# Moving the transpose of the softmax sums by one step in an attention and MLP kernel

## The chip, the cores and the metric

The kernel runs on one core of a Trainium2 chip. The metric is device time in microseconds (us) of one execution. Engines are named as in the profile: PE (TensorE matmul), PEld (TensorE weight load), DVE (VectorE), ACT (ScalarE), POOL (GpSimd), SP (SyncE, whose queue issues nearly all DMAs here).

## The reference, cut to what matters

Attention over 4 batches, 8 heads, 576 positions and head size 64, with a bias that a small network computes from the positions, and an MLP on the 2304 tokens:

```python
scores = q @ k.T / 8 + bias[head]              # 576 x 576 for each batch and head
attn = exp(scores - max(scores, axis=-1))
attn = attn / (attn.sum(axis=-1) + 1e-9)
x = concat_heads(attn @ v)                     # 2304 x 512
h = relu(x @ w_in)                             # w_in 512 x 2048
out = (s * h * h + b) @ w_out                  # w_out 2048 x 512
```

The division by the sums is what the change touches. The kernel multiplies the finished `attn @ v` by the reciprocals of the sums instead of dividing `attn`.

## The kernel before, in words

The work is written out in order by hand: every engine runs its instructions in the order of the program text, and so does SP's queue of DMAs. There are three stretches: the bias of all heads (up to about 60 us), attention (60 to 350 us), and the MLP.

**Pairs, units and steps.** Attention works on 16 pairs; a pair is one head of two batches. The query rows of a pair are five units: units 0 to 3 are 128 rows of both batches (x = 0, 1), unit 4 is the last 64 rows of both batches stacked to 128. One step per unit, `step(n)`, with n = 5p + u for pair p and unit u. A step does three things for three units. For unit n + 2: the scores (L228, PE into a PSUM tile for each x), `biased` (L242, DVE: subtract from the bias, and the row's minimum), and `expo` (L253, ACT: exp, which also adds up a column of the sums `su`). For unit n: `probs_t`, which transposes the exponentials on PE and copies them from PSUM. For pair p - 1: `av` (L333, L336), the product with v that accumulates in `xps`. The attended pair is therefore one pair behind the transposed one, and the scores are two units ahead of it. Because of this lead the scores that a step u = 3 computes are those of unit 0 of the next pair, and all nine columns of the sums of pair p are there by step u = 3.

**`probs_t` and its PSUM tiles.** Every call takes one of two buffers of `ps_t` (tile name `tps`, 128 x 512, one bank). A unit 0 to 3 has three calls: part 2 transposes a 128 x 128 block (L307, copied by ACT in L308), parts 0 and 1 transpose four blocks each (L298, copied by ACT in L303 and by DVE in L305). Unit 4 has two: part 1 transposes a block of 64 columns (L318, copied by two ACT instructions of L320), part 0 four blocks (L313, copied by DVE in L315).

**The sums.** In step u = 3 `norm` (L265, L266, DVE) adds 1e-9 and takes the reciprocal of the 128 x 9 sums, between the two `biased` of the step. `norm_t`, called at the end of part 2 of the same step, transposes the result on PE (L270) into the columns 128 to 255 of the tile whose columns 0 to 127 L308 has just been told to copy, and DVE copies it out (L272, tile `rt`). At the end of the step `norm_store` issues four small DMAs on SP (L278, L280) that write `rt` to device memory (`rs`), after the loads of the step (`load_be`, `load_q`, `load_k`). At the end of step u = 4 `norm_load` (L285) issues two DMAs that read each row back, repeated over 64 partitions (tile `rb`). `rb` is needed in step u = 4 of the next pair, where `av` of the previous pair ends: L341 (DVE) multiplies `xps` by `rb`, and L342 stores the result to `xt` in device memory.

**Filler.** After `av`, a step calls `fill` once (u odd) or twice (u even). Each call does one piece of decoding the MLP's weights: an ACT, a POOL or a DVE instruction (L373, L375, L377, L380, L383), at times a load of raw weights (L360) or a split (L392 to L395). In steps u = 0 and 1 POOL splits the next pair's q and k (L203, L204), which the scores of step u = 3 read.

**The end of attention.** Steps 78 and 79 (u = 3 and 4 of the last pair) and the steps 80 to 84, which only do `av` of the last pair, are mixed with the first work of the MLP: `att` is the next step, `xsp` a split of x (L419 ACT, L420 DVE), `h0` and `h1` the first two tiles of the MLP's first product (`expand`, L430 to L440):

```python
for work in (att, xsp, xsp, xsp, xsp, att, h0, att, h0, att,
             att, h1, wsp, wsp, att, h1, att, wsp, wsp):
    next(work)
pctx.close()
ps_ctx.close()
```

The PSUM tiles of the second product (`project`, L454) are allocated after that, in the room of `xps` and `tps`; so the first `project` comes after L341 of the last pair.

Of the kernel before, what the change touches and what calls it, by code (L numbers as in the profile page):

```python
# [26 lines left out]
def attention_moe(ctx, tc, q, k, v, w_in, w_out, dist, par, out):  # L27
# [14 lines left out]
    LAST = 5 * NP  # L42
# [144 lines left out]
    def load_q(p):  # L187
        if p < NP:
            h, b0 = pairs[p]
            qs[p] = io.tile([128, 640], F32, tag="qt", name="qt")  # L190
            nc.sync.dma_start(out=qs[p], in_=q[b0 // 2, h])

    def load_k(p):
        if p < NP:
            h, b0 = pairs[p]
            ks[p] = io.tile([128, S + 64], F32, tag="kt", name="kt")
            nc.sync.dma_start(out=ks[p], in_=k[b0 // 2, h])
# [16 lines left out]
    def scores(n):  # L214
        p, t = divmod(n, 5)
        qt, kt = qs[p], ks[p]
        c = slice(128 * t, 128 * t + 128)
        xs = range(width(n))
        ps = [ps_s.tile([128, 2, 512], F32, tag="s", name="sps") for _ in xs]
        mms = []  # L220
        for hf in range(2):
            for x in xs:
                d = slice(64 * x, 64 * x + 64) if t < 4 else slice(0, 128)
                o = hf * HALF + (64 if x == 0 else 0)
                for i, (a, b) in enumerate(((0, 0), (0, 1), (1, 0))):
                    mms.append((i, hf, x, ps[x][:, hf, 0:HALF], qt[d, a, c], kt[d, b, o:o + HALF]))
        for i, _, _, o, a, b in sorted(mms, key=lambda e: e[1::-1]):
            nc.tensor.matmul(o, a, b, start=(i == 0), stop=(i == 2))  # L228
        units[n] = (
            tp.tile([128, 2, S], F32, tag="pr", name="pr"),  # L230
            sm.tile([128, 2], F32, tag="mn", name="mn"),
            ps,
        )
        if t == 0:
            sums[p] = sm.tile([128, 9], F32, tag="su", name="su")

    def biased(n, x):
        p, t = divmod(n, 5)
        _, mn, ps = units[n]
        bias = bts[group[p]][:, t, 64 - 64 * x:64 - 64 * x + S] if t < 4 else bes[p]  # L240
        tt = tp.tile([128, S], F32, tag="tt", name="tt")
        nc.vector.tensor_tensor_reduce(  # L242
            tt.rearrange("p (a b) -> p a b", a=2), ps[x][:, :, 0:HALF],
            bias.rearrange("p (a b) -> p a b", a=2),
            -1.0 / ROOT, BIG, ALU.add, ALU.min, mn[:, x:x + 1],
        )
        tts[n, x] = tt

    def expo(n, x):
        p, t = divmod(n, 5)  # L250
        pr, mn, _ = units[n]
        col = 4 * x + t if t < 4 else 8
        nc.scalar.activation(  # L253
            pr[:, x], tts.pop((n, x)), AF.Exp, bias=mn[:, x:x + 1], scale=-1.0,
            accum_out=sums[p][:, col:col + 1])

    def width(n):
        return 2 if n % 5 < 4 else 1
# [4 lines left out]
    def norm(p):  # L263
        su = sums.pop(p)
        nc.vector.tensor_scalar(su, su, 1e-9, None, op0=ALU.add)  # L265
        nc.vector.reciprocal(su, su)  # L266
        rows[p] = su

    def norm_t(p, ps):
        nc.tensor.transpose(ps[0:9, 128:256], rows.pop(p), ident)  # L270
        rt = sm.tile([9, 128], F32, tag="rt", name="rt", bufs=2)
        nc.vector.tensor_copy(rt, ps[0:9, 128:256])  # L272
        rts[p] = rt

    def norm_store(p):
        rt = rts.pop(p)
        for x in range(2):
            nc.sync.dma_start(  # L278
                out=rs_d[p][x, 0:512].rearrange("(t j) -> t j", j=128), in_=rt[4 * x:4 * x + 4, :])
            nc.sync.dma_start(out=rs_d[p][x:x + 1, 512:S], in_=rt[8:9, 64 * x:64 * x + 64])  # L280

    def norm_load(p):
        rbs[p] = tp.tile([128, S], F32, tag="rb", name="rb", bufs=2)
        for x in range(2):
            nc.sync.dma_start(out=rbs[p][64 * x:64 * x + 64, :], in_=rs_d[p][x:x + 1, :].broadcast_to([D, S]))  # L285

    def probs_t(n, part):
        p, t = divmod(n, 5)
        pr = units[n][0]
        if p not in pts:  # L290
            pts[p] = (ptp.tile([128, 4, 2, S], F32, tag="pt", name="pt"),
                      ptp.tile([128, S], F32, tag="ptr", name="ptr"))
        pt, ptr = pts[p]
        ps = ps_t.tile([128, 512], F32, tag="t", name="tps")
        c = slice(128 * t, 128 * t + 128)
        if t < 4 and part < 2:
            for kb in range(4):
                nc.tensor.transpose(  # L298
                    ps[:, 128 * kb:128 * kb + 128],
                    pr[:, part, 64 * part + 128 * kb:64 * part + 128 * kb + 128], ident)  # L300
            o, i = pt[:, :, part, c], ps.rearrange("p (a b) -> p a b", a=4)
            if part == 0:
                nc.scalar.activation(o, i, AF.Copy)  # L303
            else:
                nc.vector.tensor_copy(o, i)  # L305
        elif t < 4:
            nc.tensor.transpose(ps[:, 0:128], pr.rearrange("p x j -> p (x j)")[:, 512:640], ident)  # L307
            nc.scalar.activation(ptr[:, c], ps[:, 0:128], AF.Copy)  # L308
            if t == 3:
                norm_t(p, ps)  # L310
        elif part == 0:
            for kb in range(4):
                nc.tensor.transpose(  # L313
                    ps[:, 128 * kb:128 * kb + 128], pr[:, 0, 128 * kb:128 * kb + 128], ident)
            nc.vector.tensor_copy(  # L315
                pt[:, :, :, 512:S], ps.rearrange("p (a x b) -> p a x b", a=4, x=2))
        else:
            nc.tensor.transpose(ps[0:64, 0:128], pr[:, 0, 512:S], ident)  # L318
            for x in range(2):
                nc.scalar.activation(  # L320
                    ptr[64 * x:64 * x + 64, 512:S], ps[0:64, 64 * x:64 * x + 64], AF.Copy)

    def av(p, kb, hf):
        h, b0 = pairs[p]
        pt, ptr = pts[p]
        vt = vals[p]
        if kb == 0 and hf == 0:
            accs[p] = ps_x.tile([128, 2, 512], F32, tag="x", name="xps")
        ps = accs[p]
        c = slice(hf * HALF, (hf + 1) * HALF)  # L330
        if kb < 4:
            for x in range(2):
                nc.tensor.matmul(ps[64 * x:64 * x + 64, hf, 0:HALF], vt[:, 4 * x + kb, :], pt[:, kb, x, c],  # L333
                                 start=(kb == 0), stop=False)
        else:
            nc.tensor.matmul(ps[:, hf, 0:HALF], vt[:, 8:10].rearrange("p i d -> p (i d)"), ptr[:, c],  # L336
                             start=False, stop=True)
        if kb == 4 and hf == 1:
            xs = rbs.pop(p)
            xv = xs.rearrange("p (a b) -> p a b", a=2)  # L340
            nc.vector.tensor_tensor(xv, ps[:, :, 0:HALF], xv, op=ALU.mult)  # L341
            nc.sync.dma_start(out=xt_d[b0 // 2][:, h * D:(h + 1) * D, :], in_=xs)  # L342
# [125 lines left out]
    def ok(n, x):  # L468
        return 0 <= n < LAST and x < width(n)
# [7 lines left out]
    def step(n):  # L477
        p, u = divmod(n, 5)
        m = n + 2
        cur = 0 <= n < LAST  # L480
        if ok(m, 0):
            scores(m)
            biased(m, 0)
        if cur and u == 3:
            norm(p)
        if ok(m, 1):
            biased(m, 1)
        if cur:
            for part in (2, 0, 1) if u < 4 else (1, 0):
                probs_t(n, part)  # L490
        if ok(m, 0):
            expo(m, 0)
        if ok(m, 1):
            expo(m, 1)
        if p >= 1:
            av(p - 1, u, 0)
            av(p - 1, u, 1)
            fill()
            if u % 2 == 0:
                fill()  # L500
        if 0 <= n < LAST:
            if u == 3:
                load_be(p + 1)
                load_q(p + 3)
                load_k(p + 3)
                norm_store(p)
            if u == 4:
                norm_load(p)
            if u < 2:
                split_qk(p + 1, u)  # L510
            if u == 4:
                load_v(p + 2)
            for e in loads_at.get((p, u), ()):
                load_bias(*e)
# [14 lines left out]
    def fill():  # L529
        next(filler, None)  # L530
# [77 lines left out]
    for e in late[0:4]:  # L608
        load_w(*e)
    att = map(step, range(LAST - 2, LAST + 5))  # L610
    xsp = map(lambda a: split_x(0, a), range(KB))
    wsp = map(lambda i: split_w(0, 1, i), range(4))
# [107 lines left out]
```

## Time and profile before

| | |
|---|---|
| median of 3 runs | 754.46 us (754.11 to 759.69) |
| profiled execution | 759.01 us, of which the core's span is 757.0 us |
| PE busy | 722.6 us, 95% of the span |
| DVE, ACT, POOL busy | 428.3, 362.5, 185.4 us |
| mean granted TensorE clock | 0.991 |
| chain that ended last | PE 81%, POOL 6%, DVE 5%, issue 4% |
| idle time of PE before L270 | 17.3 us in 16 instructions |

Starts are us from the span's start. A row of a timeline gives start, length, engine, line, operation, output<-input, how many instructions are merged, and in brackets the idle time of the engine before it and what ended it. The end of a matmul is modelled, and pipelined matmuls overlap in the rows; the distance between starts is the safer measure. A granted clock of 1.00 is 2.4 GHz, 0.5 is 1.2 GHz; a figure in between is a mixture of the two over the stretch.

### The profile page before, as it was taken

Reading aid. Unit: us, or ns where it says so; the run is one execution under the profiler, and the core shown is the slowest. Engines: PE = TensorE matmul, PEld = TensorE weight load, DVE = VectorE, ACT = ScalarE, POOL = GpSimd, SP = SyncE. Lnnn points to the kernel's source line nnn. Section 1 sums busy time; section 2 is a strip of 40 time slices with the busy share of each in tenths; the row PEclk is TensorE's granted clock in tenths of the full one; section 3 lists DMA queues with packets and bytes.
Section 4 is the critical chain, followed back from the end, with each engine's and each line's share of the span. In section 5 each row is a group of like instructions: output and inputs, shape, how many; then the busy total and the mean of one; then the engine's idle time right before and its main releaser. Section 6 shows DMA issues by size and latency. Waiting matters only on the chain.

```text
span 757.0 us, 12033 instructions
## 1 busy us (share of the span) xinstructions
PE 722.6 (95%) x4530; PEld 538.3 (71%) x4530; DVE 428.3 (57%) x794; ACT 362.5 (48%) x756; POOL 185.4 (24%) x194
## 2 busy tenths in 40 slices
PE   8978989898999999999999999999999999999998
PEld 5436666565666666666888888888888888888896
DVE  7966867687787877894369742233323333232332
ACT  7967656465666666664454432223222232222332
POOL 7990524344141252310755200000000000000000
PEclk9999999899999999999999999999999999999999
DMA  5878654545363664334012121000300002000100
GB/s 168 281 219 265 196 181 156 181 156 209 128 209 128 211 225 156 128 114 172 17 38 88 42 79 34 1 1 0 112 1 0 1 1 83 1 1 0 57 1 28
DMA packets 39817, 76.98 MB, mean 102 GB/s; under 512 B 9040, under 2 KB 12368, under 8 KB 39760
## 3 DMA queue, kind: packets, MB, share of 16 engines
q1 hardware_dynamic: 39616, 75.90, 30.7%
q8 instruction: 35, 0.57, 0.3%
q10 hardware_dynamic: 144, 0.33, 0.1%
q14 instruction: 22, 0.18, 0.1%
HBM read 55.45 MB, written 20.13 MB: 100 GB/s over the span
## 4 chain that ended last, share of the span: by engine, by line
PE 81%; POOL 6%; DVE 5%; issue 4%; DMA 2%; SPq 1%; ACT 1%; POOLq 0%; DVEq 0%
PE hps L430 26%; PE o L454 26%; PE sps L228 8%; PE xps L333 7%; PE tps L298 7%; POOL f L119 4%; DVE tt L242 3%; PE xps L336 2%; PE tps L307 1%; PE tps L313 1%; DMA raw<-in_moe_w_in_dram 1%; PE tps L318 0%; SPq L154 0%; DMA pt__110<-in_par_dram 0%; POOL kr L204 0%
## 5 line engine op out<-in xcount | busy, mean ns | idle before, releaser
L454 PE MATMUL o<-who,gt 128*128 128x512 f32 x576 | 192.4, 393 | 0.0
L430 PE MATMUL hps<-x,whi 128*128 128x512 f32 (+1 forms) x640 | 183.7, 371 | 0.0
L435 DVE SCALAR_TENSOR_TENSOR r<-r,sb 128x512 f32<-128x512 f32 (+1 forms) x80 | 56.7, 709 | 192.3 <-ACT r L434 192.3
L434 ACT ACTIVATE r<-hps 128x512 f32<-128x512 f32 (+1 forms) x80 | 44.5, 557 | 223.7 <-PE hps L430 223.7
L430 PEld LDWEIGHTS hps<-x,whi 128*128 128x128 f32 x640 | 116.9, 188 | 23.8 <-issue 0.4
L454 PEld LDWEIGHTS o<-who,gt 128*128 128x128 f32 x576 | 108.2, 188 | 24.2
L430 PE MATMUL hps<-x,wli 128*128 128x512 f32 (+1 forms) x320 | 118.7, 371 | 0.0
L253 ACT ACTIVATE pr<-tt,mn 128x576 f32<-128x576 f32 x144 | 110.2, 767 | 13.9 <-DVE mn L242 13.4
L242 DVE CUSTOM_DVE_ANT_0 tt<-sps,bt 128x576 f32<-128x576 f32 x128 | 92.3, 749 | 39.6 <-PE sps L228 34.8
L454 PE MATMUL o<-wlo,gt 128*128 128x512 f32 x288 | 113.2, 393 | 0.0
L228 PEld LDWEIGHTS sps<-kr,qr 64*128 64x128 f32 (+1 forms) x864 | 69.5, 187 | 42.1 <-DVE mn L242 16.9
L228 PE MATMUL sps<-kr,qr 64*128 64x288 f32 (+1 forms) x864 | 90.9, 313 | 6.5 <-POOL kr L204 2.9
L440 DVE SCALAR_TENSOR_TENSOR gt<-r,sb,gt 128x512 fp32r<-128x512 f32 (+1 forms) x80 | 56.3, 704 | 54.0 <-ACT gt L439 54.0
L298 PE MATMUL tps<-ident,pr 128*128 128x128 f32 x512 | 79.6, 285 | 0.9 <-ACT ptr L308 0.3
L439 ACT ACTIVATE gt<-r,sb 128x512 fp32r<-128x512 f32 (+1 forms) x80 | 54.4, 680 | 52.3 <-DVE r L435 52.3
L333 PE MATMUL xps<-pt,vt 128*64 128x288 f32 x512 | 78.4, 430 | 0.0
L298 PEld LDWEIGHTS tps<-ident,pr 128*128 128x128 f32 x512 | 58.5, 144 | 13.4 <-ACT ptr L308 9.0
L430 PEld LDWEIGHTS hps<-x,wli 128*128 128x128 f32 x320 | 60.1, 188 | 11.0
L454 PEld LDWEIGHTS o<-wlo,gt 128*128 128x128 f32 x288 | 54.1, 188 | 11.6
L305 DVE COPY pt<-tps 128x512 f32<-128x512 f32 x64 | 44.0, 688 | 17.4 <-PE tps L298 17.4
L303 ACT ACTIVATE pt<-tps 128x512 f32<-128x512 f32 x64 | 38.3, 598 | 32.0 <-PE tps L298 30.3
L375 POOL TENSOR_SCALAR full<-full 128x512 f32<-128x512 f32 x32 | 21.0, 657 | 127.0 <-ACT full L373 120.6
(69 smaller groups left out, 742.1 us busy)
## 6 DMA issues: line engine op xcount, KB each, us to landing
bias<-stg SPq DMA_DIRECT2D x36, 288.0 KB
raw<-in_moe_w_in_dram SPq DMA_DIRECT2D x16, 512.0 KB
raw<-in_moe_w_out_dram SPq DMA_DIRECT2D x16, 512.0 KB
bt<-bias SPq DMA_DIRECT2D x7, 1152.0 KB
qt<-in_q_dram SPq DMA_DIRECT2D x16, 320.0 KB
kt<-in_k_dram SPq DMA_DIRECT2D x16, 320.0 KB
vt<-in_v_dram SPq DMA_DIRECT2D x16, 320.0 KB
rb<-rs SPq DMA_DIRECT2D x32, 144.0 KB
```

The source lines that it names most:

```text
L228: nc.tensor.matmul(o, a, b, start=(i == 0), stop=(i == 2))
L242: nc.vector.tensor_tensor_reduce(tt.rearrange("p (a b) -> p a b", a=2), ps[x][:, :, 0:HALF], bias.rearrange("p (a b) -> p a b", a=2), -1.0 ...
L253: nc.scalar.activation(pr[:, x], tts.pop((n, x)), AF.Exp, bias=mn[:, x:x + 1], scale=-1.0, accum_out=sums[p][:, col:col + 1])
L298: nc.tensor.transpose(ps[:, 128 * kb:128 * kb + 128], pr[:, part, 64 * part + 128 * kb:64 * part + 128 * kb + 128], ident)
L305: nc.vector.tensor_copy(o, i)
L333: nc.tensor.matmul(ps[64 * x:64 * x + 64, hf, 0:HALF], vt[:, 4 * x + kb, :], pt[:, kb, x, c], start=(kb == 0), stop=False)
L430: nc.tensor.matmul(ps[:, 0:n], w[0, g][:, a, fc], xs_t[c, a][:, j, 0:n], start=(i == 0), stop=(i == 3 * KB - 1))
L434: nc.scalar.activation(r, ps[:, 0:n], AF.Relu)
L435: nc.vector.scalar_tensor_tensor(r, r, sb[:, 0:1], r, op0=ALU.mult, op1=ALU.mult)
L439: nc.scalar.activation(hi, r, AF.Identity, bias=sb[:, 1:2])
L440: nc.vector.scalar_tensor_tensor(lo, r, sb[:, 1:2], hi.bitcast(F32), op0=ALU.add, op1=ALU.subtract)
L454: nc.tensor.matmul(os_t[c][i], gt[:, a, tok], w[1, g][:, fo], start=(f == 0 and j == 0), stop=(f == NF - 1 and j == 2))
```

## The change: what it does

Three edits. `norm_t` moves from part 2 of unit 3 to part 1 of unit 4: it is called one step later, after the two ACT copies of L320, and writes the columns 128 to 255 of that tile. `norm` stays in step u = 3, but behind the second `biased` instead of between the two. `norm_store` moves from step u = 3 to step u = 4 (on SP now behind the store of `xt`), and `norm_load` from step u = 4 to step u = 0 of the next pair; for the last pair it stands in step 80.

```diff
@@ probs_t
             nc.scalar.activation(ptr[:, c], ps[:, 0:128], AF.Copy)
-            if t == 3:
-                norm_t(p, ps)
...
             for x in range(2):
                 nc.scalar.activation(
                     ptr[64 * x:64 * x + 64, 512:S], ps[0:64, 64 * x:64 * x + 64], AF.Copy)
+            norm_t(p, ps)
@@ step
             biased(m, 0)
+        if ok(m, 1):
+            biased(m, 1)
         if cur and u == 3:
             norm(p)
-        if ok(m, 1):
-            biased(m, 1)
...
+        if n == LAST:
+            norm_load(p - 1)
         if 0 <= n < LAST:
             if u == 3:
                 load_be(p + 1)
                 load_q(p + 3)
                 load_k(p + 3)
+            if u == 4:
                 norm_store(p)
-            if u == 4:
-                norm_load(p)
+            if u == 0 and p > 0:
+                norm_load(p - 1)
```

## Rows read from the trace of the kernel before

**Rows 1.** Groups by line: busy us, mean ns, idle before and its releaser.

```profile
L270 PE MATMUL tps<-ident,su 128*9 128x128 f32 x16 | 4.5, 283 | 17.3 <-DVE su L266 16.9 <-ACT ptr L308 0.4
L272 DVE COPY rt<-tps 9x128 f32<-9x128 f32 x16 | 4.4, 275 | 0.8 <-PE tps L270 0.8
```

**Rows 2.** Timeline of PE, pair 14 of 16, steps u = 1 and u = 3.

```profile
302.29 0.33 PE L307 MATMUL tps<-ident,pr 128*128 128x128 f32 x1
...
303.57 1.19 PE L333 MATMUL xps<-pt,vt 128*64 128x288 f32 x8
...
308.94 0.33 PE L307 MATMUL tps<-ident,pr 128*128 128x128 f32 x1
310.40 0.27 PE L270 MATMUL tps<-ident,su 128*9 128x128 f32 x1 [1.13 <-DVE su L266]
...
311.71 1.19 PE L333 MATMUL xps<-pt,vt 128*64 128x288 f32 x8
```

**Rows 3.** Timeline of all engines, the step u = 4 that follows.

```profile
313.82 0.30 PE L318 MATMUL tps<-ident,pr 128*64 128x128 f32 x1
...
313.96 0.60 PE L313 MATMUL tps<-ident,pr 128*128 128x128 f32 x4
314.16 0.45 ACT L320 ACTIVATE ptr<-tps 64x64 f32<-64x64 f32 x2 [0.91 <-PE tps L318]
...
314.39 1.14 PE L336 MATMUL xps<-ptr,vt 128*128 128x288 f32 x4
...
315.89 0.74 DVE L341 TENSOR_TENSOR rb<-xps,rb 128x576 f32<-128x576 f32 x1
```

**Rows 4.** Timeline of all engines, last pair, steps 78 and 79.

```profile
343.39 0.21 DVE L266 RECIPROCAL su<-su 128x9 f32<-128x9 f32 x1
...
343.76 0.28 ACT L308 ACTIVATE ptr<-tps 128x128 f32<-128x128 f32 x1 [0.61 <-PE tps L307]
...
344.10 0.28 PE L270 MATMUL tps<-ident,su 128*9 128x128 f32 x1 [0.37 <-ACT ptr L308]
...
347.42 0.43 ACT L320 ACTIVATE ptr<-tps 64x64 f32<-64x64 f32 x2
```

**Rows 5.** Timeline of PE: first and last of eight stretched groups of scores in steps u = 1.

```profile
95.14 1.25 PE L228 MATMUL sps<-kr,qr 64*128 64x288 f32 x12
...
318.86 1.30 PE L228 MATMUL sps<-kr,qr 64*128 64x288 f32 x12
```

**Rows 6.** Waits of PE for POOL's split of k: total us, times, longest us.

```profile
PE sps L228 <- POOL kr L204: 2.9, 4, 1.3
```

**Rows 7.** Timeline of all engines, the hand-over to the MLP.

```profile
346.56 0.21 SPq L280 DMA_DIRECT2D rs<-rt  x1
...
349.82 0.55 SPq L342 DMA_DIRECT2D xt<-rb  x1
...
352.05 1.11 SPq L285 DMA_DIRECT2D rb<-rs  x2
...
360.11 0.74 DVE L341 TENSOR_TENSOR rb<-xps,rb 128x576 f32<-128x576 f32 x1
...
361.93 0.39 PE L454 MATMUL o<-who,gt 128*128 128x512 f32 x1
```

**Rows 8.** Waits of SP's queue, 340 to 365 us: total us, times, longest us.

```profile
SPq L342 <- DMA rb<-rs: 6.5, 1, 6.5
...
SPq L285 <- DMA rs<-rt: 1.6, 1, 1.6
```

**Rows 9.** Stretches from L270 to L318: length, busy us, granted clock, DMA share, GB/s.

```profile
310.40:313.82 3.42, 3.40 (x29) 2.20 (x29) 1.36 (x4) 2.11 (x5) 1.00 (x1) 1.00 0.08 30
105.55:110.32 4.77, 4.77 (x30) 3.27 (x30) 1.98 (x5) 2.11 (x5) 0.00 (x0) 0.65 0.13 45
144.46:150.15 5.69, 5.69 (x29) 3.85 (x30) 1.98 (x5) 2.11 (x5) 0.00 (x0) 0.52 0.09 30
183.44:188.34 4.90, 4.90 (x29) 2.81 (x30) 1.35 (x4) 2.67 (x6) 1.31 (x2) 0.65 0.23 84
```

## The prediction

> **What bounds the kernel now.** I read the page first: its busy shares and its chain of waits put PE in front, and the groups by line then show what interrupts it. The group to see is L270, the transpose of the sums: sixteen matmuls of 283 ns, with 17.3 us of idle PE ahead of them [rows 1]. Then I went through the timeline of PE in attention. A step is there one unbroken sequence of scores, transposes and `av`, and only the step u = 3 has a hole. From the start of L307 to the first `av` matmul an ordinary step takes 303.57 - 302.29 = 1.28 us, a step u = 3 takes 311.71 - 308.94 = 2.77 us [rows 2]. So PE loses 1.49 us per pair, more than the 1.13 us booked as idle, because the modelled end of L307 hides a part. The releaser is the reciprocal L266, which stands behind a `biased`, which stands behind the scores of the same step. PE sets the end and attention hands over to the MLP without slack, so what a pair loses is lost at the end too, unless something else takes it back.
>
> **The hole that goes, step u = 3.** L270 leaves, and with it the wait for L266: 1.49 us per pair less on PE. `norm` behind the second `biased` delays nothing; DVE then waits for the transposes in any case. The next wait in this step is the ordinary one of L298 for the copy of the other buffer, already in the 1.28 us.
>
> **The hole that comes, step u = 4.** L270 now stands behind L318 and the two copies of L320. Is it free to run at once, since its sums were ready long before, or does it wait for copies that read other columns of its tile? The last pair tells it: L266 ended at 343.39 + 0.21 = 343.60 us, but L270 began at 344.10, that is 0.06 us after L308 had ended (343.76 + 0.28 = 344.04) [rows 4]. It waited for ACT's copy of the same tile. The Trainium skill, "PSUM — Partial Sum Buffer", section "PSUM bank collisions raise a hardware error", has the rule behind it: PSUM is to be guarded by bank and group of 32 partitions and not by address, since disjoint columns collide too. By addresses alone the sum would come out as in the first rival; by that rule, as here.
>
> So PE waits from L318 until both copies are done. Today L320 starts 314.16 - 313.82 = 0.34 us after L318 and lasts 0.45 us [rows 3]; with 0.06 us of release and 0.11 us from L270 to the next transposes, L313 starts 0.96 us after L318 instead of 0.14 us: 0.82 us per pair more on PE. Net where PE sets the pace: 1.49 - 0.82 = 0.67 us per pair. ACT must not be late: it idles 0.91 us ahead of L320 [rows 3] and gives back about a quarter of that when the step ahead gets shorter.
>
> **DVE in steps u = 4 to 1.** DVE takes over the copy L272 (0.275 us [rows 1]) ahead of L315, in its busiest stretch. More matters that `av` ends later: 314.39 + 0.82 + 1.14 = 316.35 us, so L341 starts near 316.40 instead of 315.89 [rows 3], 0.51 us later. Where DVE sets the pace, a pair therefore gains 1.49 - 0.51 = 0.98 us. This is so in eight of the pairs 2 to 15: the scores of step u = 1 are stretched there by 0.2 to 0.6 us (first and last of the eight in [rows 5]), since they wait for `biased` to free their PSUM tiles, and four times PE also waits for POOL's split of k, fed by DVE's decoding (2.9 us [rows 6]). With a later PE such waits shrink. I take 0.9 us for these eight pairs, between 0.67 and 0.98: 7.2 us. The six others get 0.67 us: 4.0 us. Pair 1 has no `av` and waits for DVE in step u = 4 anyway; its gain lies between 0.67 and 1.49 us, I take 1.0 us. Together 12.2 us.
>
> **The buffers and the queues.** L272 frees the buffer of L318 half a microsecond before the next step's first transpose wants it. On SP the four stores now stand behind the `xt` store, ahead of `load_v`; the two reads stand at the end of step u = 0 and block the queue until the stores have landed. Behind them wait raw weights, issued two items (some six steps) before use, bias and q, k for later pairs. A block of up to 4 us is covered by that lead; without it ACT would stall in its order, with up to as much per pair. In a middle pair `rb` has four steps until L341, some 13 us, which is enough.
>
> **The last pair.** Here it is not. Today the last store is issued at 346.56 and the reads at 352.05, after a wait of 1.6 us for the stores [rows 7, 8]: they land some 5.3 us after their issue. SP then waited 6.5 us for the reads [rows 8], so `rb` landed near 352.05 + 1.11 + 6.5 = 359.7 us, only 0.4 us before L341 at 360.11 [rows 7]. After the change the stores follow the `xt` store (349.82 + 0.55 us) and end near 351.6 instead of 346.8, 4.8 us later. With the same latencies `rb` lands near 364.5, L341 ends near 365.2, and the first matmul of `project`, which needs that PSUM and starts at 361.93 today, comes 3.3 us late. From below: if the reads land faster, now that the raw weights issued ahead of them are through, only the 0.82 us of every step u = 4 are lost. From above: 4.8 us. I take 3.2 us, near the same transfers' own durations.
>
> **The clock.** After three of the steps u = 3 the granted clock fell: 0.65, 0.52, 0.65 against 1.00, and the stretch from L270 to L318 took 4.77, 5.69 and 4.90 us against 3.42 [rows 9], 5.1 us too much in all. Ahead of each fall PE had waited for POOL and for L266 within one step; the other eleven pairs with a hole of this size kept 1.00. Without the second wait I expect two of the three not to fall (1.35 + 1.48 = 2.8 us); ahead of the third, POOL's wait alone was the longest of the table (1.3 us [rows 6]). From below 0, from above 5.1 us.
>
> **The sum.** In the profiled execution: 12.2 - 3.2 + 2.8 = 11.8 us, 759.01 to 747.2 us. The median is 4.55 us below that execution, about what the falls of the clock cost there, so other executions may have fewer of them; I count half: 12.2 - 3.2 + 1.4 = 10.4 us, 754.46 to **744** us.
>
> **Rivals.**
> *L270 doesn't wait in step u = 4* (0.10). Its rows are not L320's columns. Then a pair gains 1.49 - 0.11 = 1.38 us on PE, or 1.49 - 0.275 = 1.22 us where DVE leads: about 19 us, less 3.2, with 1.4 of clock 17: 737 us. Against it: the last pair's wait.
> *Little of the tail, all of the clock* (0.08). The mechanism is right, `rb` costs 0.8 us and 5.1 us come back: 12.2 - 0.8 + 5.1 = 16.5 us, 738 us.
> *The new hole is as long as the old* (0.18). ACT reaches L320 late, by its exponentials or a filler; every 0.1 us costs 1.5 us over the pairs, and from 0.6 us on the whole 9 us are gone. With half of that, and a tail of 4.8 us: 747 to 754 us. For it: ACT has no cover beyond its 0.91 us. Against: the same two exponentials stand ahead of L307 in every other step, and leave PE's 1.28 us alone.
> *Slower: the clock falls at the new hole* (0.06). Step u = 4 gets a hole between runs of transposes in all 16 pairs, after scores that wait for POOL in some. One fall costs 1.35 to 2.27 us [rows 9]; beyond seven falls in fifteen pairs the 10 us are used up, with all fifteen it is 20 to 34 us, 764 to 778 us. Against it: holes of 1.13 us kept 1.00 in eleven pairs, and the new one is shorter.
> The Trainium skill, "TensorE: Matmul & The Clock Gate", section "A second HAM failure mode: psum-queue depth-cycling", says that frequent short idles between groups of matmuls can make the clock alternate. By it, the last rival; the trace agrees only where two waits came together.
>
> **How the numbers follow.** My forecast (0.58) spans 739 to 749 us: 12.2 us with a tail of 0.8 to 4.8 us, the clock from 0 to 5.1 us, and about 2 us of error in the pairs. The range 736 to 751 leaves out a part of the first rival, the upper half of the third and the fourth, 2 in 10. About 1% (7.5 us) is what a measurement of this kernel can tell from no change. Below 746.9 us lie some 0.50 of the forecast, the first two rivals and a little of the third: 0.71 for faster. Slower by over 1% is 0.05, from the last rival. The rest, 0.24, is the same.
>
> **What would show it.** Right: no idle ahead of L298 in step u = 3; L270 between L318 and L313 with ACT L320 as its releaser, L313 0.9 to 1.0 us after L318; pairs of 16.5 to 17.2 us instead of 17.6 and more; the last L341 waiting for the reads of `rb`, `project` late behind it; fewer falls of the clock. Wrong: L313 right behind L270 without a wait, a late L320, low clocks in step u = 4, or L373 waiting for raw weights.

## The result, and the profile after

The changed kernel takes 747.57 us (median, 745.03 to 748.92); the kernel before, on the same chip, 756.91 us (754.11 to 759.69). The ratio is 0.9866, with an interval of 0.9829 to 0.9903: faster, by 1.3%. The profiled execution took 748.92 us with a span of 747.1 us, 9.9 us less than the 757.0 of before.

First the group of L270 in the changed kernel; the columns are those of [rows 1]. Its lines are numbered differently: L316 is the short transpose (L318 before), L318 its copies on ACT (L320 before), L311 the four transposes behind (L313 before), L332 `av` (L333 before), L340 the scaling with `rb` (L341 before), L410 and L418 the load and the rounding of `x`, L453 the first `project` matmuls (L454 before).

```profile
L270 PE MATMUL tps<-ident,su 128*9 128x128 f32 x16 | 4.5, 284 | 14.0 <-ACT ptr L318 14.0
```

The 17.3 us of idle PE ahead of L270 [rows 1] are 14.0 us now, and the releaser is ACT instead of the reciprocal. The sum hides that these are two different things. The timeline of PE shows the first, a step u = 3 and the step u = 4 behind it:

```profile
309.77 0.33 PE L307 MATMUL tps<-ident,pr 128*128 128x128 f32 x1
309.94 1.19 PE L298 MATMUL tps<-ident,pr 128*128 128x128 f32 x8
311.06 1.19 PE L332 MATMUL xps<-pt,vt 128*64 128x288 f32 x8
...
313.17 0.30 PE L316 MATMUL tps<-ident,pr 128*64 128x128 f32 x1
314.01 0.28 PE L270 MATMUL tps<-ident,su 128*9 128x128 f32 x1 [0.53 <-ACT ptr L318]
314.12 0.60 PE L311 MATMUL tps<-ident,pr 128*128 128x128 f32 x4
```

The hole of step u = 3 is gone: from L307 to the first `av` matmul 1.29 us, against 2.77 in [rows 2]. The new one in step u = 4 is there in every pair: L311 starts 0.95 us after L316. The second thing is the last pair, where L270 waited 6.02 of the 14.0 us. In the timeline of all engines, SP's queue (SPq) and ACT tell why:

```profile
325.66 0.33 PE L307 MATMUL tps<-ident,pr 128*128 128x128 f32 x1
...
318.21 0.25 SPq L280 DMA_DIRECT2D rs<-rt  x1
325.35 1.11 SPq L285 DMA_DIRECT2D rb<-rs  x2
326.55 1.96 SPq L410 DMA_DIRECT2D x<-xt  x4
...
330.09 1.91 ACT L418 ACTIVATE x<-x 128x512 fp32r<-128x512 f32 x3 [3.03 <-DMA x<-xt]
...
333.89 0.43 ACT L318 ACTIVATE ptr<-tps 64x64 f32<-64x64 f32 x2
334.38 0.38 PE L270 MATMUL tps<-ident,su 128*9 128x128 f32 x1 [6.02 <-ACT ptr L318]
...
351.05 0.76 DVE L340 TENSOR_TENSOR rb<-xps,rb 128x576 f32<-128x576 f32 x1 [0.73 <-DMA rb<-rs]
352.07 0.40 PE L453 MATMUL o<-who,gt 128*128 128x512 f32 x1
```

The read-back of pair 14 now stands in step 75, behind its own four stores (the last at 318.21) and ahead of the MLP's `x` loads. It went out only at 325.35, and the waits of SP's queue between 315 and 353 us put that down to the stores, 6.7 us here and 6.8 for pair 15:

```profile
SPq L285 <- DMA rs<-rt: 13.5, 2, 6.8
```

So the `x` loads came late, ACT waited for `x` in its order, its copies of the short tile stood behind, and L270 stood behind those. The kernel before had issued the `x` loads (L411) ahead of step 78, whose first transpose stood at 343.40, and ACT did not wait:

```profile
336.37 7.06 SPq L411 DMA_DIRECT2D x<-xt  x4
...
343.40 0.33 PE L307 MATMUL tps<-ident,pr 128*128 128x128 f32 x1
```

The two timelines split the 9.9 us. Up to the first transpose of step 78 the changed kernel is 343.40 - 325.66 = 17.7 us ahead. From there to the first `project` matmul it needs 352.07 - 325.66 = 26.4 us, against 361.93 [rows 7] - 343.40 = 18.5: 7.9 us given back. 17.7 - 7.9 = 9.8; the MLP behind it takes the same time (395.1 us before, 395.0 after).

Part of the 17.7 is the clock. Of the three falls of [rows 9] one is left, in the same step as a wait for POOL, as the timeline of PE shows:

```profile
136.76 0.93 PE L228 MATMUL sps<-kr,qr 64*128 64x288 f32 x10 [1.27 <-POOL kr L204]
137.63 0.45 PE L307 MATMUL tps<-ident,pr 128*128 128x128 f32 x1
```

Stretches with their granted clock (columns as in [rows 9]): step u = 3 with the fall, the same of an ordinary pair, and behind the 6 us wait of the last pair:

```profile
137.63:142.49 4.86, 4.86 (x31) 3.35 (x30) 3.03 (x8) 2.38 (x6) 0.00 (x0) 0.65 0.99 335
309.77:313.17 3.40, 3.40 (x31) 2.26 (x29) 3.11 (x9) 2.52 (x7) 0.61 (x1) 1.00 0.65 177
334.38:341.02 6.64, 6.64 (x22) 5.03 (x22) 2.06 (x4) 0.00 (x0) 0.00 (x0) 0.65 0.48 189
```

The fall costs 4.86 - 3.40 = 1.5 us where the three of before cost 5.1, so 3.6 us came back, and 17.7 - 3.6 = 14.1 us are the pairs' own. After the long wait of the last pair the clock was low once more, at 0.65; that cost is inside the 7.9.

### The profile page after: what moved, and what is told of

Its sections match the earlier page's. It is cut to its first block, busy times and chain, and to the rows that moved or that the text cites. A ratio compares the mean times of both kernels' runs of the same rounds, so it can differ in the third digit from the quotient of the medians.

```text
span 747.1 us, 12023 instructions
## 1 busy us (share of the span) xinstructions
PE 716.6 (96%) x4530; PEld 534.9 (72%) x4530; DVE 429.3 (57%) x794; ACT 363.5 (49%) x756; POOL 186.3 (25%) x194
## 4 chain that ended last, share of the span: by engine, by line
PE 81%; issue 3%; POOL 3%; ACT 2%; DVE 1%; DMA 1%; SPq 1%; DVEq 0%; ACTq 0%; POOLq 0%
PE hps L429 27%; PE o L453 27%; PE sps L228 8%; PE xps L332 7%; PE tps L298 7%; PE xps L335 2%; PE tps L307 2%; PE tps L311 1%; POOL kr L204 1%; ACT ptr L318 1%; DMA x<-xt 1%; POOL qr L204 1%; PE tps L270 1%; POOL full L374 0%; PE tps L316 0%
## 5 line engine op out<-in xcount | busy, mean ns | idle before, releaser
L453 PE MATMUL o<-who,gt 128*128 128x512 f32 x576 | 192.5, 393 | 0.0
L453 PEld LDWEIGHTS o<-who,gt 128*128 128x128 f32 x576 | 108.3, 188 | 24.1
L253 ACT ACTIVATE pr<-tt,mn 128x576 f32<-128x576 f32 x144 | 110.1, 767 | 10.3 <-DVE mn L242 9.7
L453 PE MATMUL o<-wlo,gt 128*128 128x512 f32 x288 | 113.2, 393 | 0.0
L228 PEld LDWEIGHTS sps<-kr,qr 64*128 64x128 f32 (+1 forms) x864 | 67.8, 185 | 39.6 <-issue 10.1
L228 PE MATMUL sps<-kr,qr 64*128 64x288 f32 (+1 forms) x864 | 88.3, 311 | 5.8 <-POOL kr L204 2.7
L298 PE MATMUL tps<-ident,pr 128*128 128x128 f32 x512 | 77.1, 282 | 0.3 <-ACT ptr L308 0.3
L332 PE MATMUL xps<-pt,vt 128*64 128x288 f32 x512 | 76.5, 421 | 0.0
L298 PEld LDWEIGHTS tps<-ident,pr 128*128 128x128 f32 x512 | 57.7, 142 | 11.4 <-ACT ptr L308 11.2
L453 PEld LDWEIGHTS o<-wlo,gt 128*128 128x128 f32 x288 | 54.2, 188 | 11.6
L374 POOL TENSOR_SCALAR full<-full 128x512 f32<-128x512 f32 x32 | 22.6, 705 | 115.1 <-ACT full L372 114.6
L332 PEld LDWEIGHTS xps<-pt,vt 128*64 128x64 f32 x512 | 31.5, 137 | 24.3 <-issue 10.6
L136 PE MATMUL bps<-f,pt__110 128*32 128x512 f32 x288 | 42.8, 599 | 5.3 <-POOL f L119 2.2
```

Of the source, the lines that this page charges most:

```text
L136: nc.tensor.matmul(pb[32 * c:32 * c + 32, 0:512], w2bd, fs[c][0][:, 0:8], start=True, stop=True)
L253: nc.scalar.activation(pr[:, x], tts.pop((n, x)), AF.Exp, bias=mn[:, x:x + 1], scale=-1.0, accum_out=sums[p][:, col:col + 1])
L298: nc.tensor.transpose(ps[:, 128 * kb:128 * kb + 128], pr[:, part, 64 * part + 128 * kb:64 * part + 128 * kb + 128], ident)
L453: nc.tensor.matmul(os_t[c][i], gt[:, a, tok], w[1, g][:, fo], start=(f == 0 and j == 0), stop=(f == NF - 1 and j == 2))
```

## The experiments

The ratios are against runs of the kernel before on the same chip, whose medians lay between 756.3 and 759.8 us from set to set. In the profiled executions of experiments 2, 7 and 8 the granted clock also fell in the bias stage, to 0.57 from 52 to 60 us, and attention began some 2.7 us later than in the other profiles (first transpose at 63.0 to 63.1 us against 60.2 to 60.8). Lengths within one timeline can therefore be compared between experiments better than starts.

**1. The new hole: the sums' transpose ahead of ACT's copies.** From the changed kernel:

```diff
 nc.tensor.transpose(ps[0:64, 0:128], pr[:, 0, 512:S], ident)
+nc.tensor.transpose(ps[0:9, 128:256], rows.pop(p), ident)
 for x in range(2):
     nc.scalar.activation(
...
-    nc.tensor.transpose(ps[0:9, 128:256], rows.pop(p), ident)      # in norm_t
```

> The changed kernel with L270 put right behind the short transpose of unit 4, ahead of ACT's two copies. Theory: the new hole of 0.53 us idle (0.83 us from the short transpose to L270) is the wait for those copies alone, so the four transposes start about 0.25 us after the short one instead of 0.95 us, and 15 pairs give back 0.6 to 0.7 us each where PE leads: about 8 us less than the changed kernel, near 739 us, the hand-over with its 6 us hole shortened by at most 1 us. Rival: DVE (copy of the sums, multiplication) sets the pace of steps u = 4 to 1 by now; then the hole moves to the scores of the next steps and the time stays within 2 us of the changed kernel.

It took 739.35 us (738.33 to 740.49), ratio 0.9766 (0.9733 to 0.9798). In the timeline of PE the three transposes (L315, L316 the sums, L310) follow each other without a wait:

```profile
304.88 0.30 PE L315 MATMUL tps<-ident,pr 128*64 128x128 f32 x1
305.01 0.27 PE L316 MATMUL tps<-ident,su 128*9 128x128 f32 x1
305.12 0.60 PE L310 MATMUL tps<-ident,pr 128*128 128x128 f32 x4
```

So the hole is the wait for ACT's copy of the same tile and nothing else; the transposition itself costs 0.11 us. The hand-over stays long, 24.8 us from step 78 (316.66) to `project` (341.45): in this run the first matmuls of the MLP (tile `hps`) waited 1.99 us for `x`, and `project` 2.05 us for the late `rb`.

**2. The tail: the read-back of pair 14 behind the `x` loads.** From the changed kernel:

```diff
-            if u == 0 and p > 0:
+            if u == (2 if p == NP - 1 else 0) and p > 0:
                 norm_load(p - 1)
```

> The changed kernel with the read-back of pair 15 (norm_load) in step 77 instead of 75, so that on SP it stands behind the loads of x for the MLP. Theory: the read-back waited 6.8 us for its stores and held the x loads, ACT's split of x stood waiting for them, and L270 of the last pair behind it; with the x loads issued some 6 us earlier the 6.0 us of idle PE ahead of the last L270 shrink to 0.5 to 2 us, and the time falls by 4 to 6 us, near 742 us; the pairs stay at 16.9 us. Rival: the x loads are late because their own data (the stores of xt) or buffers come late now that attention ends earlier; then the hole stays above 5 us and the time is that of the changed kernel.

741.62 us (739.47 to 743.38), ratio 0.9786 (0.9746 to 0.9826). SP's queue and the last L270 in the timeline:

```profile
318.43 6.92 SPq L410 DMA_DIRECT2D x<-xt  x4
325.45 1.10 SPq L285 DMA_DIRECT2D rb<-rs  x2
...
329.42 0.28 PE L270 MATMUL tps<-ident,su 128*9 128x128 f32 x1 [1.16 <-ACT ptr L318]
346.48 0.47 PE L453 MATMUL o<-who,gt 128*128 128x512 f32 x1 [1.44 <-DVE rb L340]
```

The `x` loads begin 8 us earlier, the wait of the last L270 falls from 6.02 to 1.16 us, and the time by 6.0 us. The hand-over (step 78 begins at 325.57) takes 20.9 us instead of 26.4. Only now does `project` wait for the last pair's `rb`, 1.44 us: the late read-back that I had predicted was hidden behind the late `x`. The 20.9 us are still 2.4 more than before. Step 78 is 0.65 us shorter, but in step 79 the four transposes start 1.57 us after the short one (0.13 us before), since ACT's copies stand behind its four roundings of `x`, and from there to `project` it takes 1.6 us more with the wait for `rb`.

**3. `norm` behind the second `biased`, alone.** From the kernel before:

```diff
             biased(m, 0)
-        if cur and u == 3:
-            norm(p)
         if ok(m, 1):
             biased(m, 1)
+        if cur and u == 3:
+            norm(p)
```

> The kernel before with one part of the change alone: norm behind the second biased, the transpose still in step u = 3. Theory: the old hole is set by the place of the reciprocal in DVE's order, so it grows by one biased, 0.68 us, in 14 or 15 pairs: about 10 us slower than before, 766 us, with more falls of the clock perhaps 770 us. Rival: the order of norm on DVE does not matter and the hole comes from elsewhere: no change.

784.51 us (783.71 to 785.63), ratio 1.0363 (1.0329 to 1.0397): slower, and by 28 us instead of some 10. The group of L270, the timeline of PE in a step u = 3, and stretches from L270 to L318 with their granted clock:

```profile
L270 PE MATMUL tps<-ident,su 128*9 128x128 f32 x16 | 4.7, 293 | 29.1 <-DVE su L266 28.7 <-ACT ptr L308 0.4
```

```profile
309.78 0.33 PE L307 MATMUL tps<-ident,pr 128*128 128x128 f32 x1
311.90 0.27 PE L270 MATMUL tps<-ident,su 128*9 128x128 f32 x1 [1.80 <-DVE su L266]
312.01 1.57 PE L298 MATMUL tps<-ident,pr 128*128 128x128 f32 x8
```

```profile
273.25:276.60 3.35, 3.35 (x29) 2.21 (x30) 1.30 (x3) 2.11 (x5) 0.00 (x0) 1.00 0.36 131
...
311.90:316.81 4.91, 4.91 (x29) 2.90 (x29) 1.57 (x3) 2.10 (x5) 0.00 (x0) 0.65 0.10 34
```

The hole grew from 1.13 to 1.80 us, as expected. What I had not expected is the clock: of the 14 pairs between the first and the last, 13 show 0.65 or 0.66 in this stretch and 4.7 to 4.9 us, and one shows 1.00 and 3.35. The thirteen sum to 63.4 us; less 13 x 3.42 that is 19 us of lost clock, and 1.4 in the first pair. The idle time ahead of L270 grew from 17.3 to 29.1 us, by 11.8. Together 32.2, less the 5.1 us of falls that the kernel before had too: 27 us, and the spans differ by 782.6 - 757.0 = 25.6.

**4. `norm` ahead of the first `biased`, alone.** From the kernel before; can the old hole be closed without moving anything to another step?

```diff
+        if cur and u == 3:
+            norm(p)
         if ok(m, 0):
             scores(m)
             biased(m, 0)
-        if cur and u == 3:
-            norm(p)
```

> The kernel before with norm ahead of the first biased and nothing else: the transpose, the stores and the reads stay where they were. Theory: the sums are then ready before the short transpose of step u = 3 is done, and only the wait for ACT's copy L308 is left, as in the last pair before (0.70 us from L307 to L270 instead of 1.46 us): 0.75 us less in 14 pairs, 10 us, and up to 3 us of clock; no loss in the hand-over, since no DMA moves: 743 to 747 us. Rival: the gain needs the later step, because the sums of unit 4 are not ready this early and DVE waits for ACT's exponentials: no gain, or slower by up to 0.5 us per pair.

756.06 us (751.24 to 758.97), ratio 0.9986 (0.9957 to 1.0016): no gain, a miss. The timeline of PE shows what took the place of the first wait:

```profile
308.71 0.33 PE L307 MATMUL tps<-ident,pr 128*128 128x128 f32 x1
309.40 0.28 PE L270 MATMUL tps<-ident,su 128*9 128x128 f32 x1 [0.37 <-ACT ptr L308]
309.52 0.60 PE L298 MATMUL tps<-ident,pr 128*128 128x128 f32 x4
310.81 0.66 PE L298 MATMUL tps<-ident,pr 128*128 128x128 f32 x4 [0.69 <-ACT pt L303]
311.39 1.19 PE L333 MATMUL xps<-pt,vt 128*64 128x288 f32 x8
```

The wait for L266 has become one of 0.37 us for ACT's copy, and behind it the fifth of the L298 waits 0.69 us for ACT's copy of the first four, in 15 pairs. L307 to `av` takes 2.68 us, against 2.77.

**5. As 4, and the sums' transpose ahead of the copy of its tile.** In the short transpose's branch of step u = 3:

```diff
             nc.tensor.transpose(ps[:, 0:128], pr.rearrange("p x j -> p (x j)")[:, 512:640], ident)
+            if t == 3:
+                nc.tensor.transpose(ps[0:9, 128:256], rows.pop(p), ident)
             nc.scalar.activation(ptr[:, c], ps[:, 0:128], AF.Copy)
...
-        nc.tensor.transpose(ps[0:9, 128:256], rows.pop(p), ident)      # in norm_t
```

> The kernel before, with the sums prepared ahead of the step's first biased score and their transpose of step u=3 right behind the short transpose, ahead of ScalarE's copy; store and read-back where they were. If moving a step later is not needed for the gain in the pairs, both holes are gone and the time is 738 to 744. Rival: the second hole of the kernel with the early sums stays, because the fifth to eighth transpose then wait for ScalarE's copy of the first four (0.69 us in 15 pairs): only the first hole of 0.37 us goes, 15 x 0.37 = 5.5 us at most, about 751 (749 to 755).

749.43 us (748.60 to 750.21), ratio 0.9865 (0.9846 to 0.9884): as the rival had it. The waits of PE still show the second hole (L297 and L302 are L298 and L303 here):

```profile
PE tps L297 <- ACT pt L302: 10.3, 15, 0.7
```

**6. As 5, with the copy of the sums on ACT.**

```diff
-        nc.vector.tensor_copy(rt, ps[0:9, 128:256])
+        nc.scalar.activation(rt, ps[0:9, 128:256], AF.Copy)
```

> As the one before, with the copy of the transposed sums by ScalarE, right behind the short copy, in place of VectorE, where it stood behind two biased scores. If VectorE's late copy is what made the fifth to eighth transpose change their PSUM bank and wait, the second hole shrinks to 0.3 us or less and the time is 736 to 742. Rival: they wait for ScalarE all the same, whose copy of the first four now starts later by the 0.27 us of the sums' copy: the hole is 0.7 to 1.0 us and the time 751 to 758.

737.95 us (736.71 to 738.62), ratio 0.9712 (0.9691 to 0.9733). In the timeline of PE the step u = 3 shows no wait (L306 is the short transpose here, L308 that of the sums, L297 the eight others, L334 `av`):

```profile
306.19 0.33 PE L306 MATMUL tps<-ident,pr 128*128 128x128 f32 x1
306.36 0.27 PE L308 MATMUL tps<-ident,su 128*9 128x128 f32 x1
306.47 1.33 PE L297 MATMUL tps<-ident,pr 128*128 128x128 f32 x8
307.73 1.19 PE L334 MATMUL xps<-pt,vt 128*64 128x288 f32 x8
```

So the second wait of 4 and 5 came with VectorE's copy, which stood behind two `biased`: with that copy on ACT it is gone. That VectorE's copy kept the first tile's PSUM buffer, and that the four transposes then went into the buffer of the first four, is how I read the wait for ACT's copy; no row names the buffer. What 6 does show is that the pairs can be nearly freed of both holes without moving a step: from L306 to `av` it is 1.54 us against 1.28 in an ordinary step, and in four pairs a wait of up to 0.5 us for the reciprocal L266 is left. The hand-over is then as short as before: 18.3 us from step 78 (321.57) to `project` (339.88), no wait of ACT for `x` and none of DVE for `rb`.

**7. Store and read-back alone a step later**, from kernel 6, as in the changed kernel.

```diff
+        if n == LAST:
+            norm_load(p - 1)
...
-                norm_store(p)
-            if u == 4:
-                norm_load(p)
+            if u == 4:
+                norm_store(p)
+            if u == 0 and p > 0:
+                norm_load(p - 1)
```

> The kernel with early sums, transpose ahead of the copy and the copy by ScalarE (738.0 us, no hole in the pairs), with the store and the read-back alone one step later, as in the changed kernel. If the changed kernel lost its time at the hand-over through the read-back of pair 14, which waits on SyncE for its own stores and holds the x loads, the x loads start some 8 us later than in that kernel (314.5) and some 6 us are lost: 744 (742 to 746). Rival: with no hole in the pairs the x loads have slack enough, or the loss came from the transposes in step u=4: 737 to 740.

744.31 us (742.27 to 745.74), ratio 0.9804 (0.9767 to 0.9841): 6.4 us slower than kernel 6, and by as much in the hand-over, 24.7 us against 18.3. SP's queue in the timeline has the changed kernel's pattern again, 7.1 us from the start of the last store to that of the read-back, and the `x` loads behind it:

```profile
315.88 0.25 SPq L279 DMA_DIRECT2D rs<-rt  x1
323.02 1.11 SPq L284 DMA_DIRECT2D rb<-rs  x2
324.18 2.00 SPq L412 DMA_DIRECT2D x<-xt  x4
```

**8. Read-back of pair 14 alone a step later**, from kernel 6, its stores where they were.

```diff
-            if u == 4:
+            if u == 4 and p != NP - 2:
                 norm_load(p)
+            if u == 0 and p == NP - 1:
+                norm_load(p - 1)
```

> The same kernel with the stores in their old step, and the read-back of pair 14 alone one step later, right ahead of the x loads. Its stores are then two steps old. If the wait for the stores is what holds the queue, it does not wait any more and costs its own 1.1 us at most: 738 (737 to 740). Rival: its place in front of the x loads is enough to lose them their time, whatever it waits for: 742 to 746.

738.91 us (738.75 to 739.28), ratio 0.9734 (0.9696 to 0.9773): within 1 us of kernel 6. The read-back stands ahead of the `x` loads as in 7, but its stores are older and it goes out as soon as the `xt` store is issued:

```profile
309.75 0.25 SPq L279 DMA_DIRECT2D rs<-rt  x1
...
315.08 1.11 SPq L284 DMA_DIRECT2D rb<-rs  x2
316.25 7.09 SPq L412 DMA_DIRECT2D x<-xt  x4
```

On SP's queue the move changed nothing against kernel 6: there too the read-back stands right behind the `xt` store and right ahead of the `x` loads (313.34 and 314.51 us), and the hand-over takes 18.3 us in both, so the equal time is no test. What tells is the comparison with 7, whose read-back stands at the same place ahead of the `x` loads but waits for its stores; the stores of pair 15 differ there as well, and with them a wait of `project` of 2.20 us for `rb`. With 2, which moves the read-back alone, the tail is clear: the wait for the stores, at the head of SP's queue and in front of the `x` loads, cost most of it, 5.5 of the 7.9 us. The 0.53 us hole is not its cause, since kernel 7 has none.

**9. Both mends, 1 and 2 together**, the two diffs above on the changed kernel.

> The changed kernel with both mends at once: the sums' transpose of step u=4 ahead of the two ScalarE copies, and the read-back of pair 14's rows in step 77 behind the x loads. If the two losses of the changed kernel are separate (0.83 us in each of 16 pairs, and 6 us of read-back held in front of the x loads), their gains add: alone they gave 8.2 us and 6.0 us below the changed kernel's 747.6, so about 733.5 (732 to 736). Rival: they overlap at the hand-over, because with the pairs gone through faster the MLP then waits for the last pair's read-back (2.05 us and 1.44 us of that wait showed in the two alone): then only one of the two tail gains is kept, 736 to 739.

737.27 us (734.50 to 738.34), ratio 0.9710 (0.9688 to 0.9732). Together they give 10.3 us where alone they gave 8.2 and 6.0: by the medians the rival. By the ratios it is 1.6% where alone they gave 1.0 and 0.8%, so the times leave the size of the overlap open. The rows show it at the hand-over: 20.8 us here, 20.9 in experiment 2, 24.8 in 1, 26.4 in the changed kernel, so what 1 gained there is not gained again. In the timeline `project` waits for the last read-back:

```profile
337.65 0.47 PE L453 MATMUL o<-who,gt 128*128 128x512 f32 x1 [2.65 <-DVE rb L340]
```

**10. Pairs 0 to 13 as in 9, pairs 14 and 15 as in 6.** The orders of both stand side by side, each under a condition on `p`; of the queue:

```diff
-            if u == 4:
+            if u == (4 if p < NP - 2 else 3):
                 norm_store(p)
-            if u == (2 if p == NP - 1 else 0) and p > 0:
+            if u == 0 and 0 < p < NP - 1:
                 norm_load(p - 1)
+            if u == 4 and p >= NP - 2:
+                norm_load(p)
```

> Pairs 0 to 13 as in the kernel with both mends (sums' transpose in step u=4 ahead of the copies), pairs 14 and 15 as in the kernel with the early sums (transpose in step u=3, copy by ScalarE, store and read-back a step earlier). If the pairs' gain and the hand-over are independent, the pairs end as early as with the mends (step 78's first transpose at 316.8 us) and the hand-over takes 18.3 us as with the early sums, not 20.8: 737.3 - 2.5 = 734.8 (733.5 to 736.5). Rival: the last two pairs lose by the early sums what the hand-over gains: 737 to 738.

735.26 us (734.82 to 735.97), ratio 0.9687 (0.9643 to 0.9731). The figure came out, the way to it only half: the hand-over took 18.3 us, but step 78 began at 320.08 instead of 316.8. In a middle pair of this execution the read-back, which had gone out 6.7 us after its last store, landed late, and the scaling (L350 here) waited for it:

```profile
264.94 0.21 SPq L282 DMA_DIRECT2D rs<-rt  x1
271.60 1.11 SPq L287 DMA_DIRECT2D rb<-rs  x2
276.69 0.76 DVE L350 TENSOR_TENSOR rb<-xps,rb 128x576 f32<-128x576 f32 x1 [2.20 <-DMA rb<-rs]
```

From that step u = 4 to the next it took 19.3 us, 2.5 more than in experiment 9. This is the fastest median of all, but the intervals of 6, 9 and 10 overlap: that 10 beats the other two is not shown. By their ratios all three beat the changed kernel by 1.5 to 1.8%.

## Why the prediction was right, and where it was not

The time was right: 744 predicted, 747.57 measured, inside 736 to 751, and faster by 1.3%. The gain was 9.3 us against 10.4 forecast; the rest of the distance is the kernel before, whose median is 756.91 us in this set and was 754.46 in the one that the forecast started from. By its steps:

**The hole that goes** was right: 1.29 us from L307 to `av`, as in the ordinary steps of [rows 2].

**The hole that comes** was right in cause and size: 0.95 us from L316 to L311 where 0.96 was forecast, released by ACT. Experiment 1 shows the cause by taking it away. Its time of 739.35 is near the 737 that the first rival gave for a transpose that does not wait, though its hand-over lost 6.3 us where that sum had 3.2; the rival itself fell, since L270 waits in all 16 pairs. The Trainium skill's rule, "PSUM — Partial Sum Buffer", section "PSUM bank collisions raise a hardware error", agrees with that: the sums' transpose writes other columns than the copies read, and waited for them all the same.

**The pairs** gave 14.1 us, where the sum had 12.2. The mechanism held. Counted from L307 of one step u = 3 to L307 of the next, less the falls of the clock, the fifteen stretches split much as the forecast had them: five gained 0.72 to 0.80 us (forecast 0.67, PE's pace), the first 1.19 (1.0), and nine gained 0.91 to 1.39 (0.9 for eight, DVE's pace); 0.24 us were lost ahead of the first. Most of the other 1.9 us lies in the nine, four of which passed the bound of 0.98.

**"`norm` behind the second `biased` delays nothing"** holds only because L270 moved in the same change; PE shows no wait for L266 any more. Alone the edit costs 28 us (experiment 3).

**The queues** are where a step failed. I wrote that a block of SP "of up to 4 us is covered by that lead", and named raw weights, bias, q and k behind it. The block was longer in every pair but the first: between 60 and 315 us SP waited 81.9 us for the stores in all, 7.4 us the longest. There the lead covered it, and no engine shows a wait for raw weights, q or k that were loaded behind it. In step 75, where it was 6.7 us, something else stood behind it: the `x` loads, with no lead at all. I had the four stores and the read-back as work on SP, but did not walk the queue for the last two pairs.

**The last pair** was right in sign and wrong in cause. The term was -3.2 us for a late `rb`; the hand-over lost 7.9 us, beyond the upper bound of 4.8, and `rb` had at most 0.73 us of it, for which VectorE waited and `project` did not. Experiments 2, 7 and 8 give the cause: the wait for the stores of pair 14 in front of the `x` loads, 5.5 us. The late `rb` is real but came second; it shows with 1.4 to 2.65 us once `x` is no longer late (experiments 2 and 9) or less so (1). What the term did hold, the late `rb` and the hole of step 79, came to 2.4 us net in experiment 2, near the 3.2; what it left out was `x`. That a middle pair's `rb` has cover enough held in the changed kernel, where VectorE shows no wait for it in the middle pairs; with shorter pairs it no longer did (0.4 us in experiment 9, 2.2 in 10).

**The clock** gave 3.6 us in the profiled execution, 2.8 forecast: two of three falls went, as written, and the one left follows a POOL wait. The fourth rival, a clock that falls at the new hole, did not happen: with its 0.53 us of idle the stretch from L316 to the next L307 takes 3.43 to 3.45 us in all 14 middle pairs, without an outlier. Experiment 3 shows the rival's mechanism at work at 1.8 us, in 13 of 14 pairs.

**The sum** for the profiled execution was 12.2 - 3.2 + 2.8 = 11.8 and became 14.1 - 7.9 + 3.6 = 9.8 us. That the sum came so near is in part luck: two gains that were set too small, by 1.9 and 0.8, covered a part of a loss that was set too small by 4.7.

## What to carry to other kernels

A change that moves stores and the read that depends on them should be walked along its queue to the end of the stage: the wait of the read stands at the head of the queue, and what counts is what is issued behind it, above all in the last rounds, where the next stage's loads follow. Before moving a small operation to a later step for its wait, look at the order inside the tile: ahead of the copy of the same PSUM tile it cost 0.11 us in the later step (experiment 1), and some 0.3 us in the earlier one once its own copy was on ACT (experiment 6). A hole of TensorE can have a second price, a clock that falls behind it: at 1.80 us that was about 1.5 us more per pair (experiment 3), so price a longer hole by more than its length.

## What the runs showed of the hardware

- Four small stores and a read that depends on them, on one queue, were 5.3 to 8.3 us apart in the last two pairs where the read waited for the stores, from the last store's issue to the read's (336.48 to 341.79 in experiment 5, 346.56 to 352.05 before [rows 7], 7.1 us in the changed kernel, 333.65 to 341.92 in experiment 2, 326.50 to 332.51 in experiment 8).
- With idle PE of 1.79 to 2.56 us ahead of the transposes (experiment 3) the granted clock was 0.65 or 0.66 in the 4.7 to 4.9 us behind it, in 13 of 14 pairs; with 0.99 to 1.19 us it fell in three pairs of fourteen [rows 9], each after a wait for POOL; behind the 0.53 us of the changed kernel in none. With the holes of the pairs gone or nearly so, in the profiles of experiments 1 and 6, the mean granted clock of the whole span was 0.998 and 0.999, against 0.991 before. The idle time does not decide it alone: in the bias stage PE waited 1.26 us for POOL, up to 50.8 or 50.6 us, and 0.65 us for ACT behind it both in experiment 2 and in the changed kernel, and from 52 to 60 us the granted clock was 0.57 in the one and 1.00 in the other.
- A late copy of a small part of a PSUM tile was dear: 0.27 us of copy, placed behind two `biased` on VectorE, came with a wait of 0.69 us of TensorE in 15 pairs (experiments 4 and 5); when ScalarE made it, right behind its other copy, that wait was gone and the kernel 11.5 us faster (experiment 6).
